# A fused attention and MLP kernel on one core gets a newly drawn order of work

## The chip, the cores and the metric

The kernel runs on one core of a Trainium2 chip. A core has five engines with instruction streams of their own: TensorE (PE, matrix products into the eight PSUM banks; its weight loads are shown as PEld), VectorE (DVE), ScalarE (ACT), GpSimd (POOL) and SyncE (SP). Each works through its stream in order and waits on semaphores where it needs another engine's result. The metric is device time in microseconds (us), lower is better. The median before is 210.59 us over three runs, from 210.03 to 211.24.

## The reference

Two stages follow each other. The first is a linear attention with decay: for each of 4 batches and 8 heads, 768 tokens of 64 elements are worked in blocks with a running state.

```python
intra = np.einsum('bhic,bhjc->bhij', qb, kb) * Dmask[None]
intra = np.einsum('bhij,bhjd->bhid', intra, vb)
inter = np.einsum('bhid,bhde->bhie', qb * lam_pow[None], kv_state)
out[:, :, sl] = intra + inter
kv_state = lam_block * kv_state + np.einsum('bhsd,bhse->bhde', kb * rev_pow, vb)
```

The second is an MLP on the 3072 tokens of 512 elements that come out, with 2048 hidden elements:

```python
h = x @ w_in
s = np.sin(alpha * h)
g = h + s * s / (alpha + 1e-09)
return (g @ w_out).astype(np.float32)
```

Inputs and output are float32 in memory; loads by POOL cast to bfloat16, and products accumulate in float32.

## The kernel before, in words

The tokens are cut into six tiles of 128 positions, each taken over all four batches: 512 rows to the MLP. A fixed opening (lines 148 to 454) loads tile 0 and works its attention. After it the whole program is a text of some 660 words, ORDER (line 16), which a loop (line 491) reads word by word; each word calls one step and so appends its instructions to the engines' streams. The order of the words is therefore the order on each engine; nothing reorders it later. A digit after a colon names the PSUM bank or banks that the step writes. The next user of a bank waits until its last reader is done.

The words, with t for a tile (g where the MLP uses it), f for a hidden block of 128 (0 to 15), m for a batch:

- Loads, issued by POOL: `I` (w_in, 512 of 2048 columns, two transfers, L141), `W` (w_out, a quarter, one transfer, L145), `r` and `R` (k and q of a tile in the layout that is to be turned, four transfers each, L124), `v` and `n` (v and k in natural layout, two transfers each, L131). r and R have a single buffer; the next load waits until the tile before is turned. w_in quarter 0 is loaded by the opening.
- POOL work: `d` (decay of k, L260), `z` (scaling of q, L264), `C` (cast of the first state).
- DVE work on the attention: `k`, `j` (turn k and q, L240), `m` (mask the scores, L255), `S` (new state, L283; tile 0's on ACT).
- PE work on the attention: `F` (scores, L249), `K` (state products, L274), `O` (outputs, L295 and L304).
- ACT work on it: `x` (copy of the outputs into the MLP's input, L314), `B` (cast of a state).
- The MLP: `h` (four matmuls for a hidden block, L325), `s` (sine on ACT, L330), `q` or `Q` or `P` (its square: on ACT, L336; on DVE as tensor_tensor, L338; on DVE as a three-operand operation, L340), `t` (DVE adds the scaled square to h from PSUM and writes g, which frees the bank, L345), `u` (four of the 16 matmuls of an output tile of 128 rows: `u0.1.2` is tile 0, batch 1, hidden blocks 8 to 11, L352), `o` (copy to SBUF on ACT, L358, and the store through SP, L360).

A tile's h need its four x; its u with part p need the t of blocks 4p to 4p+3 and w_out quarter p. The result blocks g of only two tiles exist at a time, so the first t of a tile waits for all u of the tile two before. After the last word, a call (line 494) makes the last output tile, tile 5 of batch 3, in two halves of 256 columns (L367), each copied (L371) and stored on its own.

Of the kernel before, what the change touches and what calls it, by code (L numbers as in the profile page):

```python
# [13 lines left out]


ORDER = """
I1 W0 d0.0 I2 h0.0:2 d0.1 h0.1:4 s0.0 h0.2:5 s0.1 Q0.0 I3 t0.0 K0:73 s0.2 Q0.1 h0.3:6 S0.0 r1 t0.1 q0.2 C0.0
h0.4:0 s0.3 t0.2 S0.1 h0.5:1 q0.3 h0.6:2 C0.1 s0.4 t0.3 s0.5 h0.7:7 R1 q0.4 u0.0.0:4 q0.5 t0.4 s0.6 u0.1.0:5
t0.5 s0.7 Q0.6 h0.8:3 t0.6 h0.9:6 Q0.7 s0.8 t0.7 h0.10:0 s0.9 Q0.8 t0.8 W1 h0.11:1 s0.10 Q0.9 W2 h0.12:2 t0.9
q0.10 s0.11 v1 t0.10 h0.13:7 s0.12 k1.0 h0.14:3 q0.11 q0.12 t0.11 h0.15:6 s0.13 W3 t0.12 s0.14 u0.2.0:0 k1.1  # L20
q0.13 z1.0 u0.3.0:1 q0.14 t0.13 s0.15 t0.14 q0.15 z1.1 j1.0 u0.0.1 t0.15 u0.1.1 j1.1 F1.0:2736 R2 u0.2.1 m1.0.0
m1.0.1 u0.0.2 m1.0.2 u0.1.2 m1.0.3 r2 F1.1:2736 u0.3.1 m1.1.0 m1.1.1 u0.2.2 m1.1.2 u0.3.2 m1.1.3 O1:2736 v2
u0.0.3 x1.0 x1.1 u0.1.3 x1.2 x1.3 u0.2.3 z2.0 o0.0 o0.1 h1.0:2 o0.2 h1.1:7 s1.0 z2.1 j2.0 h1.2:3 q1.0 k2.0 s1.1
h1.3:6 s1.2 n1 t1.0 h1.4:4 q1.1 k2.1 q1.2 u0.3.3 s1.3 t1.1 s1.4 h1.5:5 n2 t1.2 o0.3 h1.6:0 q1.4 P1.3 s1.5 t1.4
F2.0:2713 s1.6 t1.3 r3 h1.7:4 q1.5 m2.0.0 q1.6 h1.8:6 m2.0.1 s1.7 m2.0.2 u1.0.0:2 q1.7 m2.0.3 s1.8 d1.0 u1.1.0:7
t1.5 q1.8 h1.9:1 t1.6 t1.7 d1.1 h1.10:3 s1.9 t1.8 h1.11:5 q1.9 j2.1 s1.10 h1.12:0 d2.0 s1.11 t1.9 q1.10 K1:46
s1.12 t1.10 h1.13:1 d2.1 q1.12 S1.0 h1.14:3 s1.13 S1.1 B1.0 u1.0.1 t1.12 B1.1 R3 q1.13 Q1.11 K2:46 t1.11 s1.14
h1.15:0 t1.13 q1.14 u1.1.1 S2.0 s1.15 v3 u1.0.2 t1.14 q1.15 B2.0 S2.1 F2.1:5143 t1.15 B2.1 u1.1.2 m2.1.0 n3
u1.0.3 m2.1.1 m2.1.2 z3.0 u1.1.3 o1.0 m2.1.3 u1.2.0:6 o1.1 k3.0 O2:0514 z3.1 j3.0 k3.1 u1.3.0:2 x2.0 x2.1 j3.1
u1.2.1 x2.2 x2.3 F3.0:3705 h2.0:1 m3.0.0 m3.0.1 h2.1:4 s2.0 m3.0.2 h2.2:3 q2.0 m3.0.3 s2.1 t2.0 h2.3:7 s2.2 d3.0  # L30
u1.3.1 q2.1 q2.2 t2.1 h2.4:0 s2.3 t2.2 d3.1 h2.5:5 q2.3 s2.4 t2.3 h2.6:1 s2.5 r4 q2.4 K3:43 q2.5 t2.4 h2.7:7
s2.6 t2.5 h2.8:0 q2.6 S3.0 R4 s2.7 h2.9:5 t2.6 B3.0 s2.8 h2.10:4 Q2.7 t2.7 s2.9 h2.11:1 S3.1 q2.8 v4 q2.9 u1.2.2
t2.8 B3.1 t2.9 h2.12:7 s2.10 k4.0 s2.11 u1.3.2 n4 q2.10 k4.1 u1.2.3 q2.11 s2.12 u1.3.3 t2.10 o1.2 t2.11 q2.12
z4.0 F3.1:3054 o1.3 t2.12 u2.0.0:6 m3.1.0 h2.13:1 m3.1.1 z4.1 u2.0.1 m3.1.2 s2.13 m3.1.3 h2.14:2 j4.0 O3:7305
s2.14 Q2.13 q2.14 t2.13 t2.14 u2.0.2 x3.0 d4.0 j4.1 x3.1 h2.15:4 x3.2 x3.3 F4.0:1273 s2.15 d4.1 h3.0:0 m4.0.0
q2.15 m4.0.1 h3.1:5 s3.0 t2.15 h3.2:1 q3.0 m4.0.2 s3.1 t3.0 K4:24 s3.2 m4.0.3 u2.0.3 q3.1 S4.0 q3.2 h3.3:7 t3.1
o2.0 B4.0 u2.1.0:0 t3.2 r5 s3.3 S4.1 F4.1:3265 q3.3 u2.1.1 m4.1.0 B4.1 m4.1.1 h3.4:1 R5 m4.1.2 u2.1.2 m4.1.3
s3.4 t3.3 h3.5:4 q3.4 t3.4 v5 O4:3265 s3.5 k5.0 q3.5 u2.1.3 x4.0 t3.5 x4.1 k5.1 h3.6:7 x4.2 x4.3 h3.7:1 z5.0
o2.1 s3.6 u2.2.0:3 s3.7 h3.8:4 q3.6 z5.1 j5.0 q3.7 u2.2.1 s3.8 t3.6 F5.0:2650 q3.8 t3.7 u2.2.2 t3.8 h3.9:7
m5.0.0 m5.0.1 u2.2.3 s3.9 m5.0.2 h3.10:1 q3.9 m5.0.3 o2.2 u2.3.0:4 t3.9 s3.10 j5.1 h3.11:2 q3.10 t3.10 u2.3.1  # L40
s3.11 q3.11 F5.1:6503 u2.3.2 t3.11 m5.1.0 h3.12:7 m5.1.1 u2.3.3 m5.1.2 s3.12 m5.1.3 h3.13:1 q3.12 o2.3 t3.12
O5:2650 s3.13 q3.13 t3.13 u3.0.0:3 h3.14:4 u3.0.1 s3.14 h3.15:7 q3.14 t3.14 u3.0.2 x5.0 x5.1 h4.0:1 x5.2 x5.3
h4.1:4 s3.15 h4.2:2 s4.0 q3.15 h4.3:6 q4.0 t3.15 h4.4:5 s4.1 t4.0 s4.2 u3.0.3 q4.1 q4.2 h4.5:0 t4.1 o3.0 t4.2
u3.1.0:7 s4.3 s4.4 h4.6:1 q4.3 u3.1.1 q4.4 t4.3 s4.5 h4.7:4 t4.4 s4.6 u3.1.2 q4.5 q4.6 t4.5 h4.8:3 s4.7 t4.6
u3.1.3 q4.7 s4.8 t4.7 h4.9:2 o3.1 q4.8 u3.2.0:6 s4.9 t4.8 h4.10:5 q4.9 u3.2.1 t4.9 s4.10 u4.0.0:0 q4.10 t4.10
u3.2.2 h4.11:1 u3.2.3 s4.11 u4.0.1 q4.11 o3.2 t4.11 h4.12:4 u4.0.2 s4.12 h4.13:7 q4.12 t4.12 h4.14:3 s4.13
u4.1.0:2 q4.13 s4.14 t4.13 h4.15:5 q4.14 u4.1.1 t4.14 s4.15 h5.0:6 q4.15 t4.15 u4.1.2 s5.0 u4.0.3 q5.0 u4.1.3
o4.0 h5.1:1 o4.1 u3.3.0:4 s5.1 u4.2.0:7 q5.1 u3.3.1 h5.2:3 u3.3.2 s5.2 u4.2.1 q5.2 u3.3.3 h5.3:5 t5.0 o3.3
u4.2.2 t5.1 s5.3 t5.2 h5.4:0 q5.3 t5.3 u4.2.3 s5.4 h5.5:2 q5.4 o4.2 t5.4 u4.3.0:4 s5.5 h5.6:6 q5.5 t5.5 u4.3.1
s5.6 h5.7:1 q5.6 t5.6 u4.3.2 s5.7 h5.8:3 q5.7 t5.7 u4.3.3 s5.8 h5.9:5 q5.8 o4.3 t5.8 h5.10:7 s5.9 u5.0.0:0 q5.9  # L50
s5.10 t5.9 h5.11:2 q5.10 u5.0.1 t5.10 s5.11 h5.12:6 q5.11 t5.11 h5.13:1 s5.12 u5.0.2 q5.12 s5.13 t5.12 h5.14:4
q5.13 u5.1.0:3 t5.13 s5.14 h5.15:5 q5.14 t5.14 u5.1.1 s5.15 u5.2.0:7 q5.15 t5.15 u5.1.2 u5.0.3 u5.1.3 o5.0
u5.2.1 o5.1 u5.2.2 u5.2.3 o5.2
"""


# [1 line left out]
def kernel(  # L58
# [273 lines left out]
    def square(g, f, eng):  # L332
        s_sb = s_of.pop((g, f))
        s2_of[g, f] = mlps.tile([P, GRP], BF16, name="s2")
        if eng is A:
            A.activation(out=s2_of[g, f][:], in_=s_sb[:], func=ACTF.Square)  # L336
        elif eng is V:
            V.tensor_tensor(out=s2_of[g, f][:], in0=s_sb[:], in1=s_sb[:], op=ALU.mult)  # L338
# [9 lines left out]
    def project(g, m, part, n):  # L348
        if part == 0:
            ops[g, m] = bank("ops", n)  # L350
        for f in range(4 * part, 4 * part + 4):
            nc.tensor.matmul(out=ops[g, m][:], lhsT=gall[g][:, f, m * P:(m + 1) * P],  # L352
                             rhs=w_out_sb[part][:, f % 4, :],
                             start=(f == 0), stop=(f == NFC - 1))
# [170 lines left out]
```

## Time and profile before

| | us |
|---|---|
| median of three runs | 210.59 |
| the profiled execution, its own time | 212.47 |
| its span, first to last instruction | 210.8 |
| PE busy | 197.1 (94%) |
| DVE busy | 135.7 (64%) |
| ACT busy | 148.1 (70%) |
| POOL busy | 100.8 (48%) |
| last matmul ends | 207.57 |

The mean granted TensorE clock is 0.991 of full speed. POOL's own queue of loads moves 15.47 MB in 63184 packets; in the profile's 40 slices of 5.3 us the DMA engines are busy at nine tenths or more in twelve of the first thirteen. Busy time of PE is modelled for overlapping matmuls, so the waits and the order of time say more than the share. A row of a timeline gives start and length in us, engine, line, operation, tiles and a count; in brackets is the idle time ahead of it with what ended that.

### The profile page before, as it was taken

What the parts mean: (1) busy time and instruction counts of PE and PEld (TensorE: products, weight loads), DVE (VectorE), ACT (ScalarE), POOL (GpSimd) and SP (SyncE); (2) the same over time, 40 slices, a digit from 0 to 9 for tenths busy, and PEclk for the clock granted to TensorE, in tenths of its full rate; (3) what the DMA queues carried; (4) which work ended last, traced back from release to release, by engine and by line L of the source; (5) the groups of instructions that cost most, each with busy time, mean ns of one, the idle gap of its engine ahead of it and who ended that gap; (6) DMA issues with size and microseconds to landing.
All of it is one profiled execution on the core that took longest, in us unless ns stands there. A gap on an engine that the chain in (4) does not pass through costs nothing.

```text
span 210.8 us, 4860 instructions
## 1 busy us (share of the span) xinstructions
PE 197.1 (94%) x1992; PEld 97.7 (46%) x2021; DVE 135.7 (64%) x201; ACT 148.1 (70%) x258; POOL 100.8 (48%) x116
## 2 busy tenths in 40 slices
...
GB/s 124 156 151 182 205 193 162 165 197 166 229 165 166 77 145 183 48 142 157 157 75 166 116 53 50 51 2 0 53 50 50 0 100 35 70 16 33 0 105 98
DMA packets 68920, 22.61 MB, mean 107 GB/s; under 512 B 50834, under 2 KB 65954, under 8 KB 68898
## 3 DMA queue, kind: packets, MB, share of 16 engines
q0 software_dynamic: 63184, 15.47, 79.6%
...
q14 instruction: 6, 0.05, 0.1%
...
## 4 chain that ended last, share of the span: by engine, by line
PE 74%; DMA 11%; DVE 5%; POOL 4%; ACT 2%; issue 2%; DVEq 0%; ACTq 0%; POOLq 0%
PE ops L352 35%; PE hps L325 29%; DMA w_in<-in_moe_w_in_dram 4%; DMA w_out<-in_moe_w_out_dram 4%; DMA nat_k<-in_k_dram 3%; PE F_ps L249 3%; PE O_ps L304 2%; DVE gall L345 2%; POOL nat_k L260 2%; DVE STm L255 2%; PE hps L367 2%; PE O_ps L295 2%; POOL w_in L141 1%; DVE S L283 1%; PE T_ps L387 1%
## 5 line engine op out<-in xcount | busy, mean ns | idle before, releaser
L345 DVE SCALAR_TENSOR_TENSOR gall<-s,r_sb,hps 128x512 bf16<-128x512 bf16 x96 | 69.3, 742 | 46.9 <-ACT s L336 36.8
L325 PE MATMUL hps<-xt,w_in 128*128 128x512 bf16 x372 | 90.9, 379 | 2.0 <-issue 0.7
L352 PE MATMUL ops<-w_out,gall 128*128 128x512 bf16 x352 | 88.1, 382 | 4.0 <-DMA w_out<-in_moe_w_out_dram 2.4
L330 ACT ACTIVATE s_sb<-hps,alpha_sb 128x512 bf16<-128x512 f32 x96 | 64.2, 692 | 27.7 <-PE hps L325 27.5
L325 PEld LDWEIGHTS <-w_in 128*128 128x128 bf16 x384 | 36.7, 98 | 46.0 <-issue 2.2
L352 PEld LDWEIGHTS <-gall 128*128 128x128 bf16 x368 | 35.1, 98 | 44.8 <-issue 3.7
L336 ACT ACTIVATE s<-s_sb 128x512 bf16<-128x512 bf16 x86 | 52.9, 638 | 1.6
L255 DVE TENSOR_TENSOR STm<-F_ps,C 128x512 bf16<-128x512 f32 x40 | 25.0, 683 | 4.2 <-PE F_ps L249 4.1
L260 POOL TENSOR_TENSOR nat_k<-nat_k,R 128x1024 bf16<-128x1024 bf16 x10 | 19.1, 1933 | 4.5 <-DMA nat_k<-in_k_dram 4.4
L264 POOL TENSOR_TENSOR raw_q<-raw_q,Rraw 128x1024 bf16<-128x1024 bf16 x10 | 18.9, 1919 | 4.0 <-DMA raw_q<-in_q_dram 4.0
L314 ACT CAST xt<-O_ps 128x512 bf16<-128x512 f32 x20 | 10.3, 600 | 14.9 <-PE O_ps L304 14.5
L358 ACT COPY o_sb<-ops 128x512 f32<-128x512 f32 x23 | 13.5, 592 | 8.0 <-PE ops L352 6.2
L240 DVE STREAM_TRANSPOSE turned_q<-raw_q 128x512 f32<-128x512 f32 x10 | 11.1, 1114 | 5.6 <-POOL raw_q L264 5.6
L131 POOL DMA_DIRECT2D nat_v<-in_v_dram x12 | 14.0, 1170 | 0.2 <-issue 0.2
L124 POOL DMA_DIRECT2D raw_k<-in_k_dram x20 | 11.7, 598 | 3.9 <-DMA w_out<-in_moe_w_out_dram 2.9
L124 POOL DMA_DIRECT2D raw_q<-in_q_dram x20 | 11.6, 588 | 4.0 <-DMA w_in<-in_moe_w_in_dram 2.6
L131 POOL DMA_DIRECT2D nat_k<-in_k_dram x10 | 11.8, 1190 | 0.8 <-POOLq L509 0.8
L240 DVE STREAM_TRANSPOSE turned_k<-raw_k 128x512 f32<-128x512 f32 x10 | 11.0, 1117 | 0.1
L338 DVE TENSOR_TENSOR s<-s_sb 128x512 bf16<-128x512 bf16 x9 | 5.9, 657 | 2.4 <-ACT s_sb L330 2.4
L249 PEld LDWEIGHTS <-turned_k 32*128 32x128 bf16 x320 | 5.0, 96 | 4.6 <-issue 3.8
L249 PE MATMUL F_ps<-turned_q,turned_k 32*128 32x128 bf16 x320 | 6.8, 224 | 0.0
L192 PE MATMUL spare<-fill 128*128 128x512 bf16 x11 | 5.0, 607 | 1.5 <-DVE one L174 1.5
...
## 6 DMA issues: line engine op xcount, KB each, us to landing
...
```

Source lines behind the costliest of these rows:

```text
L124: (eng or G).dma_start(out=dst[quad[a], bs].rearrange("t b n r d -> t (b n) (r d)"), in_=src[t, a])
L131: G.dma_start(out=nat[nm, t][:, bs].rearrange("p b h e -> p (b h) e"), in_=SRC[nm][bs, :, t * T:(t + 1) * T, :].rearrange("b h p e -> p (b ...
L240: V.transpose(out=dst.rearrange("p (x t r) -> p x r t", r=R, t=32), in_=src.rearrange("p (x r d) -> p x r d", r=R, d=32))
L249: nc.tensor.matmul(out=F[a][:, u, n, :], lhsT=KQ["k", t][quad[a], 2 * pr + u, n, :, e], rhs=KQ["q", t][quad[a], 2 * pr + u, n, :, e], star ...
L255: V.tensor_tensor(out=st[t, pr][:, a], in0=att["F", pr][a], in1=C0[:, a].unsqueeze(1).broadcast_to([P, 2, NQ, T]), op=ALU.mult)
L260: G.tensor_tensor(out=kd, in0=kd, in1=R128[:].unsqueeze(1).unsqueeze(3).broadcast_to([P, 2, H, D]), op=ALU.mult)
L264: G.tensor_tensor(out=qs, in0=qs, in1=Rraw[:].rearrange("p n r -> p (n r)").unsqueeze(1).unsqueeze(3).broadcast_to([P, 2, NQ * R, D]), op= ...
L325: nc.tensor.matmul(out=hps[g, f][:], lhsT=w_in_sb[f // 4][:, c, (f % 4) * P:(f % 4 + 1) * P], rhs=xt[g][:, c, :], start=(c == 0), stop=(c ...
L330: A.activation(out=s_of[g, f][:], in_=hps[g, f][:], func=ACTF.Sin, scale=alpha_sb[:, f:f + 1])
L336: A.activation(out=s2_of[g, f][:], in_=s_sb[:], func=ACTF.Square)
L345: V.scalar_tensor_tensor(out=gall[g][:, f, :], in0=s2_of.pop((g, f))[:], scalar=r_sb[:, f:f + 1], in1=hps.pop((g, f))[:], op0=ALU.mult, op ...
L352: nc.tensor.matmul(out=ops[g, m][:], lhsT=gall[g][:, f, m * P:(m + 1) * P], rhs=w_out_sb[part][:, f % 4, :], start=(f == 0), stop=(f == NF ...
```

## The change

The table ORDER is another one, drawn by annealing over nine sets of disturbed durations. It has the same steps with the same numbers, so the same loads, matmuls, masks, sines, copies and stores, in other places and with other banks. The kinds of square differ: ACT had 86, DVE had 9 as tensor_tensor and 1 as three-operand operation; now ACT has 52, DVE 35 and 9. The output tile in halves becomes a word, `e5.3:14`, which gives its two banks; it still stands last. The fixed opening is untouched.

Of the diff, the start of both tables, the new part around tile 3's end, the new end, and the code:

```diff
 ORDER = """
-I1 W0 d0.0 I2 h0.0:2 d0.1 h0.1:4 s0.0 h0.2:5 s0.1 Q0.0 I3 t0.0 K0:73 s0.2 Q0.1 h0.3:6 S0.0 r1 t0.1 q0.2 C0.0
-h0.4:0 s0.3 t0.2 S0.1 h0.5:1 q0.3 h0.6:2 C0.1 s0.4 t0.3 s0.5 h0.7:7 R1 q0.4 u0.0.0:4 q0.5 t0.4 s0.6 u0.1.0:5
-t0.5 s0.7 Q0.6 h0.8:3 t0.6 h0.9:6 Q0.7 s0.8 t0.7 h0.10:0 s0.9 Q0.8 t0.8 W1 h0.11:1 s0.10 Q0.9 W2 h0.12:2 t0.9
-q0.10 s0.11 v1 t0.10 h0.13:7 s0.12 k1.0 h0.14:3 q0.11 q0.12 t0.11 h0.15:6 s0.13 W3 t0.12 s0.14 u0.2.0:0 k1.1
-q0.13 z1.0 u0.3.0:1 q0.14 t0.13 s0.15 t0.14 q0.15 z1.1 j1.0 u0.0.1 t0.15 u0.1.1 j1.1 F1.0:2736 R2 u0.2.1 m1.0.0
...
+h0.0:0 s0.0 I1 h0.1:2 s0.1 h0.2:6 s0.2 P0.0 q0.1 Q0.2 t0.0 t0.2 h0.3:7 s0.3 h0.4:4 q0.3 t0.3 t0.1 I2 h0.5:5
+h0.6:0 d0.1 h0.8:3 h0.7:2 s0.4 q0.4 t0.4 h0.10:4 s0.5 q0.5 d0.0 t0.5 s0.6 Q0.6 t0.6 s0.7 s0.8 P0.7 t0.7 Q0.8
+h0.9:5 s0.9 K0:70 Q0.9 t0.9 S0.0 I3 R1 W0 S0.1 s0.10 W1 t0.8 q0.10 t0.10 r1 W2 h0.11:1 s0.11 Q0.11 t0.11 h0.13:2
+W3 z1.0 h0.12:6 s0.12 s0.13 h0.14:5 q0.12 P0.13 z1.1 t0.12 h0.15:0 u0.1.0:7 s0.14 q0.14 u0.3.0:1 C0.1 u0.0.0:6
+u0.2.0:4 t0.13 j1.0 s0.15 q0.15 u0.3.1 t0.15 u0.0.1 j1.1 u0.2.1 k1.0 u0.1.1 t0.14 k1.1 F1.0:0532 u0.2.2 m1.0.2
+m1.0.0 v1 m1.0.1 m1.0.3 u0.1.2 u0.3.2 F1.1:0532 C0.0 m1.1.3 m1.1.1 u0.3.3 o0.3 u0.2.3 o0.2 m1.1.2 u0.0.2 m1.1.0
+O1:0345 x1.0 x1.1 u0.0.3 x1.3 x1.2 r2 k2.0 k2.1 u0.1.3 o0.1 R2 h1.0:5 s1.0 h1.1:1 h1.2:0 Q1.0 t1.0 o0.0 s1.1
+Q1.1 t1.1 s1.2 Q1.2 h1.3:4 t1.2 s1.3 q1.3 h1.4:6 h1.5:7 s1.4 s1.5 n1 t1.3 v2 h1.8:3 q1.4 q1.5 n2 z2.0 j2.0
...
+m3.0.2 m3.0.0 z3.1 u1.2.3 x2.3 h2.0:0 s2.0 m3.0.1 j3.1 Q2.0 t2.0 d3.0 h2.1:1 s2.1 q2.1 m3.0.3 h2.2:6 t2.1 h2.4:2
+h2.3:5 s2.2 s2.3 Q2.2 t2.2 s2.4 h2.5:4 o1.2 u1.3.0:1 Q2.3 h2.6:7 u1.3.1 Q2.4 t2.3 s2.5 d3.1 q2.5 v3 s2.6 q2.6
+t2.4 h2.7:3 F3.1:5026 s2.7 t2.5 q2.7 m3.1.1 h2.8:4 t2.6 u1.3.2 s2.8 q2.8 m3.1.3 h2.9:7 R4 s2.9 q2.9 u1.3.3
+m3.1.0 m3.1.2 K3:06 t2.7 S3.1 t2.9 o1.3 t2.8 B2.0 S3.0 r4 k4.0 h2.10:2 s2.10 z4.0 j4.0 h2.11:1 s2.11 O3:7356
+q2.10 q2.11 t2.10 t2.11 x3.0 x3.1 x3.2 u2.0.0:4 x3.3 h2.12:0 s2.12 Q2.12 t2.12 u2.0.1 F4.0:7652 m4.0.2 m4.0.3
...
+t5.14 u5.1.0:7 u5.2.2 u5.1.1 t5.15 u5.0.3 o5.0 u5.1.2 u4.0.0:0 u5.1.3 o5.1 u4.3.3 o4.3 u5.2.3 o5.2 u4.0.1 u4.0.2
+u4.0.3 o4.0 e5.3:14
 """
...
-    def project_halves(g, m):
+    def project_halves(g, m, *bks):
...
-            ps = bank("hps", n)
+            ps = bank("ops", bks[n])
...
+        "e": project_halves,
     }
     for word in ORDER.split():
         which, _, banks = word[1:].partition(":")
         STEP[word[0]](*map(int, which.split(".")), *map(int, banks))
-    project_halves(NT - 1, B - 1)
```

Of what the prediction names and the cut does not show: before, r4 stood ahead of R4 and v4, and v3 ahead of n3; the new order of loads from tile 3 on is R3 n3 z3 d3 v3 R4 r4 z4 n4 v4 d4 R5 r5 z5 v5.

More of the change, by code (lines that the diff above doesn't have):

```diff
@@ L22 @@
[L22 to L51, printed above, removed]
@@ L52 @@
-q5.13 u5.1.0:3 t5.13 s5.14 h5.15:5 q5.14 t5.14 u5.1.1 s5.15 u5.2.0:7 q5.15 t5.15 u5.1.2 u5.0.3 u5.1.3 o5.0
-u5.2.1 o5.1 u5.2.2 u5.2.3 o5.2
+h0.0:0 s0.0 I1 h0.1:2 s0.1 h0.2:6 s0.2 P0.0 q0.1 Q0.2 t0.0 t0.2 h0.3:7 s0.3 h0.4:4 q0.3 t0.3 t0.1 I2 h0.5:5
+h0.6:0 d0.1 h0.8:3 h0.7:2 s0.4 q0.4 t0.4 h0.10:4 s0.5 q0.5 d0.0 t0.5 s0.6 Q0.6 t0.6 s0.7 s0.8 P0.7 t0.7 Q0.8
+h0.9:5 s0.9 K0:70 Q0.9 t0.9 S0.0 I3 R1 W0 S0.1 s0.10 W1 t0.8 q0.10 t0.10 r1 W2 h0.11:1 s0.11 Q0.11 t0.11 h0.13:2
+W3 z1.0 h0.12:6 s0.12 s0.13 h0.14:5 q0.12 P0.13 z1.1 t0.12 h0.15:0 u0.1.0:7 s0.14 q0.14 u0.3.0:1 C0.1 u0.0.0:6
```

22 lines of the change are left out of this document (added).

## The prediction

> **What bounds the kernel now.** I read the busy shares first, then TensorE's groups, then TensorE in order of time, then clock and DMA by the microsecond, and last the single DMA issues.
>
> ```profile
> PE 197.1 (94%) x1992; PEld 97.7 (46%) x2021; DVE 135.7 (64%) x201; ACT 148.1 (70%) x258; POOL 100.8 (48%) x116
> ```
>
> TensorE (PE) is the only engine near its span. Its two large groups show what could still be won:
>
> ```profile
> L325 PE MATMUL hps<-xt,w_in 128*128 128x512 bf16 x372 | 90.9, 379 | 2.0 <-issue 0.7
> L352 PE MATMUL ops<-w_out,gall 128*128 128x512 bf16 x352 | 88.1, 382 | 4.0 <-DMA w_out<-in_moe_w_out_dram 2.4
> ```
>
> The last columns are idle time ahead of the group: little, and its largest piece is a wait for a w_out load. In order of time (start, length, matmuls):
>
> ```profile
> 34.21 1.89 PE L352 MATMUL ops<-w_out,gall 128*128 128x512 bf16 x8
> 38.49 2.37 PE L352 MATMUL ops<-w_out,gall 128*128 128x512 bf16 x8 [2.39 <-DMA w_out<-in_moe_w_out_dram]
> ...
> 42.16 3.04 PE L352 MATMUL ops<-w_out,gall 128*128 128x512 bf16 x11 [0.34 <-issue]
> ...
> 52.70 4.48 PE L325 MATMUL hps<-xt,w_in 128*128 128x512 bf16 x20
> ```
>
> Behind the wait the same matmuls are slower: eight took 2.37 us, against 1.73 in the chain. The rows by the microsecond say why (after the window: PE, PEld, DVE, ACT, POOL busy, then granted clock, DMA share, GB/s):
>
> ```profile
> 37.00:38.00 1.00, 0.00 (x0) 0.00 (x0) 0.51 (x1) 0.06 (x1) 1.00 (x2) 1.00 0.98 146
> ...
> 40.00:41.00 1.00, 1.00 (x14) 0.22 (x16) 0.44 (x1) 0.00 (x0) 0.27 (x1) 0.50 2.36 158
> 41.00:42.00 1.00, 0.82 (x32) 0.69 (x26) 0.15 (x1) 0.00 (x0) 1.00 (x3) 0.50 2.44 163
> 42.00:43.00 1.00, 0.84 (x2) 0.29 (x2) 1.00 (x2) 0.00 (x0) 1.00 (x2) 0.50 2.03 180
> ```
>
> The clock stood at half from about 39.2 to 43.1. Late in the run the chain is unbroken matmuls:
>
> ```profile
> 162.55 1.73 PE hps L325 x8
> 164.28 0.86 PE ops L352 x4
> ```
>
> So an h or u word of the table (four matmuls) costs 0.86 us of PE. By the chain an F is 0.57, an O 0.69 + 1.01 = 1.70, a K 0.62.
>
> **The ledger of before.** Words ahead of h1.0: 16 h, 15 u, K0, two F, O1, or 30.2 us. PE ran its first h at 16.79 and h1.0 at 52.70, 35.9 us; so 5.7 were lost: 2.39 for W1, some 1.7 at half clock (0.64 and 0.67 in the two rows above, 0.4 in the F between), the rest in short waits for w_in, K0 and banks. From h1.0 on there are 152.8 us of words and 154.87 us until 207.57, when PE ends: 2.1 lost, about 1.4 of it in gaps of 0.05 to 0.16 marked issue. The 3.2 us left are the last copy and store. The change removes no matmul, so it acts on 5.7 and 2.1 alone.
>
> **The change, part one: the opening.** The table moves W0 from between I1 and I2 to behind R1, and W1, W2 and W3 ahead of v1. POOL now issues I1, I2, d0.1, d0.0, I3, R1, W0, W1, r1, W2, W3, z1.0, z1.1, C0.1, v1, C0.0, r2. In PE's order every h0 and K0 now stands before the first u.
>
> Landing times come from the single DMA issues of before, in us: I1 21.3, W0 23.6, I2 27.3, I3 29.6, r1 32.2, R1 34.9, W1 38.5, W2 41.5, v1 45.0, W3 47.6. The transfers follow each other without a gap: a w_in pair costs 2.3 (27.3 to 29.6), four raw loads 2.6, a w_out 2.6 to 3.6 (I take 3.2), a nat pair 3.5. POOL's issues wait only for the load eight issues back (a raw_k issue at 23.8 went when W0 landed), which fits here. From I1 at 21.3 the new sequence gives I2 23.7, I3 26.1, R1 28.7, W0 32.0, W1 35.2, r1 37.8, W2 41.0, W3 43.8, v1 47.3.
>
> PE against that, each word 0.86: h0.0 at 16.79; h0.2 waits 0.2 for the second half of w_in (18.7); h0.4 waits 0.9 for I1; then 12 h and K0 (banks freed in time by rows of 0.70 per sine, 0.63 per square, 0.66 per finish) end at 32.3, when W0 is there. Eight u end at 39.4, behind W1. F1.0 waits 0.2 for DVE (z1.0 done 31.6, then j1.0, t0.15, j1.1, k1.0 after r1, t0.14); u0.2.2 waits 0.8 for W2; F1.1 waits 0.1 for masks. W3 and v1 are in time for u0.3.3 and O1. After O1 (48.5) four x copies (2.05 in before) hold h1.0's third matmul, 0.3. That is some 2.4 lost against 5.7: gain 3.3. No wait is above 0.9, so I take no clock drop. Bounds: with w_out at 3.6 each, and a square that meets z1.1 (below), 2.0; with 2.6 each, 4.2. I take 3.3, since 3.2 is the middle of the four w_out.
>
> The Trainium skill (TensorE: Matmul & The Clock Gate, Part 1) puts the drop after an idle window of about 3.4 us. This trace disagrees: 2.39 us sufficed. By that page the half clock would not belong to the W1 wait and the gain would be an estimated 1.6; I go by the row.
>
> **Part two: squares move from ACT to DVE.** Squares on ACT (q) fall from 86 to 52, on DVE as tensor_tensor (Q) they rise from 9 to 35, as the three-operand form (P) from 1 to 9. ACT sheds 34 x 0.615 = 21 us, DVE takes 26 x 0.42 + 8 x 0.68 = 16 us. After tile 3 both have room. Between h1.0 and h3.0 DVE's words sum to about 52 us beside 51 us of PE (before: 51 beside 53), so there the cover is gone. The price of a Q is not fixed:
>
> ```profile
> L338 DVE TENSOR_TENSOR s<-s_sb x9: 418/419/1824, 18.6 to 103.1; 128x512 bf16<-128x512 bf16 x9
> ```
>
> The 1.82 one began at 18.57, 0.4 after a POOL tensor_tensor (18.17 to 20.10), and ended as that one did; one at 103.06 took 1.16 beside another. Beside DMA issues it stays at 0.42. So a Q that meets a z or d loses up to 1.4. In the new order that can happen to Q0.11 (z1), Q1.2 (z2.0, about 55), Q2.0 (d3), Q3.7 (z5). Each delays DVE, and PE only where a bank is due: from 0 to 1.9 in all; I take 0.5. Denser bank reuse (h1.6 to u1.0.0 after 2.3 us of PE, where sine, square and finish need 0.69 + 0.63 + 0.75 + 0.2) adds 0 to 0.9; I take 0.3.
>
> **Part three: later loads.** r4 moves from ahead of R4 to behind v3 and R4, while k4.0 stands on DVE ahead of j4.0, t2.10 and t2.11, which F4.0 awaits. POOL after d3.1 (about 83.0) issues v3, R4, r4 until 90.0. From an empty queue n1 and n2 of before (54.7 to 59) took 5.5 us to the first landing, then 1.7 to 2.6 each, raw 0.65 to 1.0 each: r4 lands between 96.2 and 98.2. DVE is ready near 95.5 and PE wants F4.0 at 98.7; k4.0, j4.0 and t2.10 take 2.8, so F4.0 waits 0.3 to 2.3. I take 0.8, nearer the lower, which starts from an empty queue as here. K4 (d4.0 done 108 to 111, wanted 111.3) and F5.0 have little room: 0 to 1; I take 0.1.
>
> **Part four: the end.** project_halves becomes word e5.3 with banks 1 and 4 in place of 0 and 1; four u4.0 parts stand just ahead of it where u5.2 stood. Same matmuls, copies, stores: 0, bounds 0.3 either way.
>
> **Sum.** -3.3 + 0.5 + 0.3 + 0.8 + 0.1 = -1.6. The profiled execution took 212.47 (span 210.8 and 1.67 around it), so it would take 210.9; it lies 1.88 above the median of 210.59, so that I predict 209.0.
>
> **Rivals.**
> 1. All later terms hidden, since PE still has 152 us of words that banks may cover: 210.59 - 3.3 = 207.3. For it: DVE idles 4.7 us at 48 to 53 in before. Against: DVE was without a pause from 62 to 82.
> 2. DVE becomes the bound from tile 1 to 3: two or three squares meet POOL's operations at 1.4 each with nothing idle behind, 2.0 more than I took, and 210.9 or so. For it: 52 beside 51 us; against: 0.42 is what seven of nine took. The Trainium skill (SBUF — State Buffer, SBUF: two separate sides) extends the lock to any DVE operation with two SBUF inputs, so to P; no row here shows it for P.
> 3. Slower: r4 comes late. d3.0 waits for n3, v3 and R4 queue behind d3.1, r4 behind both, k4.0 blocks DVE, and PE stands at F4.0. Each us past 95.9 costs one. From a landing at 99.4 the kernel is over 0.5% slower; at 100 it takes 4.1 instead of 0.8 and gives 212.3. For it: R4 and r4 cost 4.0 and 3.1 us in before when the queue had run empty (issues at 88.7 and 86.35), against the 2.6 of the opening; against: the queue is empty when v3 goes.
>
> **How the numbers follow.** Within 0.5% means 209.5 to 211.6, about what a measurement can tell from no change. Forecast: 0.42 (its own range 207.9 to 210.2; 0.32 faster, 0.10 same). Rival 1: 0.22, faster. Rival 2: 0.16 (0.02 faster, 0.12 same, 0.02 slower). Rival 3: 0.20 (0.17 slower, 0.03 same). Sum: 0.56 faster, 0.25 same, 0.19 slower. The range runs from 206.8, half a us inside rival 1 with the opening's better bound (207.3 less part of the 0.9 between 3.3 and 4.2), to rival 3 at 212.3; it leaves out about 1 in 10 on either side.
>
> **What would show it.** Right: no wait of PE above 1 us for w_out, no clock row at 0.50 between 30 and 50, W0 landing near 32 and W3 near 44, h1.0 at about 50.5; r4 landing by 97 and F4.0 at about 99.5; about 165 us of large matmuls unchanged. Wrong: a new half-clock row, h1.0 after 52, DVE without a pause from 52 to 105 with several Q near 1.8, or F4.0 more than 2 us behind u2.0.1.

## The result, and the profile after

The changed kernel takes 222.75 us in the median of six runs (220.75 to 226.02), the kernel before beside it 210.57 (209.55 to 211.24). The ratio is 1.056, with a 95% interval of 1.050 to 1.061: 12 us slower, where the prediction said 209.0. Runs of one kernel scatter here, some by several per cent, so every ratio below compares undisturbed runs alone, and a median stands beside its range.

The profiled execution took 222.6 us with a span of 220.8, so it stands for the median. Its busy shares and its costliest groups:

```profile
PE 198.2 (90%) x1995; PEld 97.3 (44%) x2021; DVE 159.4 (72%) x235; ACT 130.4 (59%) x224; POOL 101.0 (46%) x116
L325 PE MATMUL hps<-xt,w_in 128*128 128x512 bf16 x372 | 91.5, 386 | 10.3 <-DVE gall L345 7.4
L352 PE MATMUL ops<-w_out,gall 128*128 128x512 bf16 x355 | 85.8, 380 | 3.9 <-DVE gall L345 2.6
L338 DVE TENSOR_TENSOR s<-s_sb 128x512 bf16<-128x512 bf16 x35 | 25.7, 736 | 13.1 <-ACT s_sb L330 12.9
```

Over the whole run TensorE's matmuls cost nearly what they did (386 and 380 ns in the mean against 379 and 382). New are 10.3 us of idle time ahead of the h group, most of it ended by DVE's finish (t, L345), and a square on DVE that takes 736 ns in the mean where 420 were reckoned. The answer for line 338 gives least, median and most in ns:

```profile
L338 DVE TENSOR_TENSOR s<-s_sb x35: 404/424/6152, 20.2 to 198.4; 128x512 bf16<-128x512 bf16 x35
```

So the usual square did cost 0.42, and one took 6.15. TensorE in order of time (in brackets the idle time ahead of a row and what ended it):

```profile
32.84 1.02 PE L352 MATMUL ops<-w_out,gall 128*128 128x512 bf16 x4
36.18 1.02 PE L352 MATMUL ops<-w_out,gall 128*128 128x512 bf16 x4 [2.32 <-DVE gall L345]
...
52.79 6.21 PE L325 MATMUL hps<-xt,w_in 128*128 128x512 bf16 x28
66.38 3.57 PE L325 MATMUL hps<-xt,w_in 128*128 128x512 bf16 x8 [7.39 <-DVE gall L345]
```

Eight matmuls of h took 3.57 us behind the long wait, against 1.73 in the unbroken chain. The windows show why (after the window: PE, PEld, DVE, ACT, POOL busy, then granted clock, DMA share, GB/s):

```profile
55.00:60.00 5.00, 4.00 (x19) 1.71 (x18) 5.00 (x1) 2.59 (x5) 5.00 (x3) 1.00 2.13 205
60.00:65.00 5.00, 0.00 (x0) 0.00 (x0) 4.89 (x6) 2.41 (x4) 4.60 (x6) 0.70 2.30 173
65.00:70.00 5.00, 3.62 (x16) 1.10 (x19) 3.85 (x6) 1.32 (x3) 3.19 (x2) 0.50 1.06 114
70.00:75.00 5.00, 4.78 (x47) 2.41 (x45) 3.61 (x6) 3.64 (x7) 0.61 (x1) 0.77 0.01 1
```

DVE is busy for the whole of 55 to 60 with one instruction, POOL with three. In order of time, the rows of DVE and POOL around both waits of TensorE (rows of other engines are left out):

```profile
31.28 3.77 POOL L264 TENSOR_TENSOR raw_q<-raw_q,Rraw 128x1024 bf16<-128x1024 bf16 x2
31.55 3.79 DVE L338 TENSOR_TENSOR s<-s_sb 128x512 bf16<-128x512 bf16 x1
...
54.58 6.15 DVE L338 TENSOR_TENSOR s<-s_sb 128x512 bf16<-128x512 bf16 x1 [2.18 <-ACT s_sb L330]
54.76 1.97 POOL L264 TENSOR_TENSOR raw_q<-raw_q,Rraw 128x1024 bf16<-128x1024 bf16 x1
56.63 1.96 POOL L260 TENSOR_TENSOR nat_k<-nat_k,R 128x1024 bf16<-128x1024 bf16 x1
58.49 1.95 POOL L264 TENSOR_TENSOR raw_q<-raw_q,Rraw 128x1024 bf16<-128x1024 bf16 x1
60.33 2.35 POOL L124 DMA_DIRECT2D raw_k<-in_k_dram  x4
61.43 1.34 DVE L338 TENSOR_TENSOR s<-s_sb 128x512 bf16<-128x512 bf16 x1
```

The square of 3.79 us is Q0.11. It lies beside z1.0 and z1.1, which follow each other without a pause, and ends 0.29 behind them. The one of 6.15 is Q1.0, beside z2.0, d1.0 and z2.1, and ends 0.29 behind the third, while POOL issues DMAs. Behind Q1.0 on DVE stand t1.0, Q1.1, t1.1, Q1.2, t1.2 and t1.3; the last frees bank 4 for h1.6.

How tight that is can be counted. TensorE has 28 matmuls (h1.0 to h1.5 and h1.8) before it needs bank 4, and stood still from 58.99. From Q1.0's start at 54.58 that is a cover of 4.4 us. At the usual prices DVE needs 3 x 0.42 + 4 x 0.75 = 4.3 us for these seven words. It took 11.8 (to 66.34), and 11.8 - 4.4 is the wait of 7.4. There was next to no slack (0.1), so nearly every microsecond on DVE was one on TensorE.

**The ledger.** After h1.0 the kernel has 151.9 us of words (0.86 less than before, since one more u now stands ahead of h1.0). It took from 52.79 to 217.53, so 12.8 were lost where the profiled execution of before lost 2.1: 7.4 in the wait, some 1.8 in the row of 65 to 70 (half of 3.62) and 1.1 in that of 70 to 75 (0.23 of 4.78) by the clock, the rest in short gaps. Ahead of h1.0 the same u shifts before's 52.70 to 53.56, so the opening won 0.8 of the 3.3 forecast. The sum, 10.7 - 0.8 = 9.9, is the difference of the spans (10.0).

### The profile page after: what moved, and what is told of

Read it like the earlier page. It is cut to its first block, busy times and chain, and to the rows that moved or that the text cites. A ratio compares the mean times of both kernels' runs of the same rounds, so it can differ in the third digit from the quotient of the medians.

```text
span 220.8 us, 4860 instructions
## 1 busy us (share of the span) xinstructions
PE 198.2 (90%) x1995; PEld 97.3 (44%) x2021; DVE 159.4 (72%) x235; ACT 130.4 (59%) x224; POOL 101.0 (46%) x116
## 4 chain that ended last, share of the span: by engine, by line
PE 67%; POOL 12%; DMA 12%; issue 3%; DVE 3%; ACT 0%; POOLq 0%; ACTq 0%; DVEq 0%
PE hps L325 30%; PE ops L352 30%; DMA nat_k<-in_k_dram 5%; DMA raw_k<-in_k_dram 4%; DMA w_in<-in_moe_w_in_dram 3%; POOL w_in L141 2%; PE F_ps L249 2%; POOL nat_v L131 2%; POOL nat_k L131 2%; PE O_ps L304 2%; PE ops L367 2%; POOL raw_k L124 2%; POOL nat_k L260 2%; PE O_ps L295 1%; PE KV_ps L274 1%
## 5 line engine op out<-in xcount | busy, mean ns | idle before, releaser
L325 PE MATMUL hps<-xt,w_in 128*128 128x512 bf16 x372 | 91.5, 386 | 10.3 <-DVE gall L345 7.4
L352 PE MATMUL ops<-w_out,gall 128*128 128x512 bf16 x355 | 85.8, 380 | 3.9 <-DVE gall L345 2.6
L345 DVE SCALAR_TENSOR_TENSOR gall<-s,r_sb,hps 128x512 bf16<-128x512 bf16 x96 | 68.7, 738 | 13.7 <-ACT s L336 12.6
L325 PEld LDWEIGHTS <-w_in 128*128 128x128 bf16 x384 | 37.2, 99 | 55.6 <-issue 13.3
L338 DVE TENSOR_TENSOR s<-s_sb 128x512 bf16<-128x512 bf16 x35 | 25.7, 736 | 13.1 <-ACT s_sb L330 12.9
L336 ACT ACTIVATE s<-s_sb 128x512 bf16<-128x512 bf16 x52 | 31.8, 628 | 1.0
L131 POOL DMA_DIRECT2D nat_k<-in_k_dram x10 | 11.8, 1186 | 1.5 <-POOLq L509 0.8
L340 DVE SCALAR_TENSOR_TENSOR s<-s_sb 128x512 bf16<-128x512 bf16 x9 | 7.0, 776 | 3.3 <-ACT s_sb L330 3.3
L283 DVE SCALAR_TENSOR_TENSOR S<-S,L,KV_ps 128x512 f32<-128x512 f32 x8 | 6.0, 745 | 3.3 <-PE KV_ps L274 3.3
(68 smaller groups left out, 101.4 us busy)
```

The costliest lines, as they stand in the source:

```text
L131: G.dma_start(out=nat[nm, t][:, bs].rearrange("p b h e -> p (b h) e"), in_=SRC[nm][bs, :, t * T:(t + 1) * T, :].rearrange("b h p e -> p (b ...
L325: nc.tensor.matmul(out=hps[g, f][:], lhsT=w_in_sb[f // 4][:, c, (f % 4) * P:(f % 4 + 1) * P], rhs=xt[g][:, c, :], start=(c == 0), stop=(c ...
L345: V.scalar_tensor_tensor(out=gall[g][:, f, :], in0=s2_of.pop((g, f))[:], scalar=r_sb[:, f:f + 1], in1=hps.pop((g, f))[:], op0=ALU.mult, op ...
```

## The experiments

The theories have letters in the expectations. **L**: a DVE square gets no turn while POOL's tensor_tensor operations follow each other without a pause (such a row is called a train below). Rivals are **W** (DVE simply has too much work), **D** (the later loads hold DVE and PE), **M** (only the two-operand form is held up) and, later, **O** (what the edited kernels still lack is lost in a stretch at half clock in the opening) and **S** against **T** (whether the wait for W1 is what put the profiled execution of before above the median, or is in every execution). The edits change only words of ORDER, so each kernel computes everything.

### Tile 1's three squares to ACT

```diff
-O1:0345 x1.0 x1.1 u0.0.3 x1.3 x1.2 r2 k2.0 k2.1 u0.1.3 o0.1 R2 h1.0:5 s1.0 h1.1:1 h1.2:0 Q1.0 t1.0 o0.0 s1.1
-Q1.1 t1.1 s1.2 Q1.2 h1.3:4 t1.2 s1.3 q1.3 h1.4:6 h1.5:7 s1.4 s1.5 n1 t1.3 v2 h1.8:3 q1.4 q1.5 n2 z2.0 j2.0
+O1:0345 x1.0 x1.1 u0.0.3 x1.3 x1.2 r2 k2.0 k2.1 u0.1.3 o0.1 R2 h1.0:5 s1.0 h1.1:1 h1.2:0 q1.0 t1.0 o0.0 s1.1
+q1.1 t1.1 s1.2 q1.2 h1.3:4 t1.2 s1.3 q1.3 h1.4:6 h1.5:7 s1.4 s1.5 n1 t1.3 v2 h1.8:3 q1.4 q1.5 n2 z2.0 j2.0
```

> The changed kernel with the squares Q1.0, Q1.1 and Q1.2 as q (on ACT), nothing else. Theory L (a DVE square with two SBUF inputs gets no turn while POOL's tensor_tensor operations follow each other without a pause): the 6.15 us square is gone, with it PE's wait of 7.39 us and the half clock behind it (about 3 us), so 211 to 214 us. Rival W (DVE simply has too much work in tiles 1 to 3, wherever POOL is): 1.3 us of DVE work are taken away, so 220 to 222 us. Rival D (the later loads hold DVE and PE): no change, 222 to 223 us.

Measured: 216.07 us (213.66 to 216.81), ratio 1.024 (1.016 to 1.031). The long wait shrank from 7.39 to 1.25, and the clock stayed at 1.00 from 60 to 70:

```profile
62.26 1.89 PE L325 MATMUL hps<-xt,w_in 128*128 128x512 bf16 x8 [1.25 <-DVE gall L345]
```

Three words of 660 give back 6.7 of the 12.2 us. L forecast 211 to 214, so it was 2 us too hopeful. Of this h1.6's wait accounts for 1.25: ACT now does three squares more among its sines, and each finish ahead of it waited for one of them. The opening was slower too: in this trace h1.0 starts only at 54.80, 2.0 later than in the changed kernel's, though no word ahead of it differs: Q0.11 took 3.40 us here too (TensorE waited 2.35), and the granted clock was 0.72 from 15 to 20 and 0.77 from 35 to 40, where the changed kernel's trace has 1.00. So one execution's opening can differ from another's by some 2 us, and a single trace prices it no better than that.

### Tile 0's one square to ACT

```diff
-h0.9:5 s0.9 K0:70 Q0.9 t0.9 S0.0 I3 R1 W0 S0.1 s0.10 W1 t0.8 q0.10 t0.10 r1 W2 h0.11:1 s0.11 Q0.11 t0.11 h0.13:2
+h0.9:5 s0.9 K0:70 Q0.9 t0.9 S0.0 I3 R1 W0 S0.1 s0.10 W1 t0.8 q0.10 t0.10 r1 W2 h0.11:1 s0.11 q0.11 t0.11 h0.13:2
```

> The changed kernel with the one square Q0.11 as q. L: the 3.79 us square beside z1.0 and z1.1 goes, PE's wait of 2.32 us ahead of u0.3.0 too: 220 us or less; since tile 1 then starts some 2 us earlier, its first squares may run ahead of z2.0, and then it can be down to 212. W: 0.4 us of DVE work less, 222 us. D: 222 to 223 us.

Measured: 221.12 us (218.84 to 226.88), ratio 1.042 (1.034 to 1.049). By the ratio (1.042 of 210.59 is 219.4) L's 220 or less is met. The profiled execution was the longest of the four (226.88), so its rows show what can happen and not what the median is made of. With Q0.11 gone, the next square on DVE, P0.13, ran into z1.1 and took 2.19 in place of 0.68. Q1.0 took 7.26:

```profile
53.34 7.26 DVE L338 TENSOR_TENSOR s<-s_sb 128x512 bf16<-128x512 bf16 x1 [1.76 <-ACT s_sb L330]
54.65 1.96 POOL L264 TENSOR_TENSOR raw_q<-raw_q,Rraw 128x1024 bf16<-128x1024 bf16 x1
```

Here Q1.2 met a second train as well, of three decays, and took 5.15; TensorE waited 12.22 us. One square less on DVE thus left others in POOL's operations: where a square meets one is a matter of a microsecond.

### All four to ACT

The two edits together.

> The changed kernel with Q0.11, Q1.0, Q1.1 and Q1.2 as q. L: both trains of POOL operations meet no square any more, 12 us come back: 209 to 211.5 us, no row of granted clock at 0.50 after the opening. W: 219 to 222 us. D: 221 to 223 us.

Measured: 213.75 us (211.64 to 215.47), ratio 1.011 (1.004 to 1.019). h1.0 starts at 51.17, and behind the wait for h1.6 TensorE has no idle time to speak of until the end:

```profile
58.63 1.89 PE L325 MATMUL hps<-xt,w_in 128*128 128x512 bf16 x8 [1.25 <-DVE gall L345]
```

Ahead of h1.0 one wait of 1.50 us is left, and it is P0.13 again (2.14 us beside z1.1). So four words carry 9 of the 12 us, though L's figure (209 to 211.5) is missed by about 2; the profiled execution took 211.64. All other moves of the table, tile 3's late loads (rival 3) and DVE's load between tile 1 and 3 (rival 2) among them, are left in this kernel and show no wait.

### The kernel before, with one square on DVE

The fault planted in the other order, at the word that stands ahead of POOL's three decays there:

```diff
-F2.0:2713 s1.6 t1.3 r3 h1.7:4 q1.5 m2.0.0 q1.6 h1.8:6 m2.0.1 s1.7 m2.0.2 u1.0.0:2 q1.7 m2.0.3 s1.8 d1.0 u1.1.0:7
+F2.0:2713 s1.6 t1.3 r3 h1.7:4 q1.5 m2.0.0 q1.6 h1.8:6 m2.0.1 s1.7 m2.0.2 u1.0.0:2 Q1.7 m2.0.3 s1.8 d1.0 u1.1.0:7
```

> The kernel before with one square, q1.7, as Q1.7 on DVE, where POOL runs four decays without a pause (61.6 to 69.1 us). L: the square starts near 63.5 and ends only at about 69.4, some 5.9 us; PE runs out of banks for 3 to 6 us and may lose up to 2 more at half clock: 214 to 219 us. W: 0.42 us of DVE work more, 210.5 to 211.5 us. D: no change.

Measured: 212.49 us in ten runs (210.46 to 221.5), ratio 1.003 (0.998 to 1.009). The mechanism is there in the profiled run, of 213.83 us; its price in the time can't be told from nothing, and L's figure is missed:

```profile
60.19 4.13 DVE L338 TENSOR_TENSOR s<-s_sb 128x512 bf16<-128x512 bf16 x1
60.22 5.86 POOL L260 TENSOR_TENSOR nat_k<-nat_k,R 128x1024 bf16<-128x1024 bf16 x3
```

The square ended 0.29 behind the second of three decays, and not behind the third. The profile shows no pause between them: the third starts at 63.95, as the second ends, and takes 2.12 in place of 1.9. So here the square got its turn inside a train, which L does not allow, and the decay seems to have waited instead. The trace of before has such a case as well: its square at 103.06 ended 0.29 behind the first of two decays (102.03 to 103.93), and the second, from 103.94, took 2.03. More of them stand under part two below. A mask and four finishes stood behind the square on DVE, and in this execution TensorE waited 2.63 us for the mask and 0.85 for a finish, waits that neither trace of the unedited kernel has.

### POOL's train split, squares left on DVE

Only POOL's words move: z2.0 ahead of the load n2, and the load r3 up to n2, so that z2.0 and the decays are parted by DMA issues. All squares stay as in the changed kernel.

```diff
-Q1.1 t1.1 s1.2 Q1.2 h1.3:4 t1.2 s1.3 q1.3 h1.4:6 h1.5:7 s1.4 s1.5 n1 t1.3 v2 h1.8:3 q1.4 q1.5 n2 z2.0 j2.0
+Q1.1 t1.1 s1.2 Q1.2 h1.3:4 t1.2 s1.3 q1.3 h1.4:6 h1.5:7 s1.4 s1.5 n1 t1.3 v2 h1.8:3 q1.4 q1.5 z2.0 n2 r3 j2.0
...
-t1.10 s1.13 z2.1 j2.1 t1.11 q1.12 t1.12 h1.14:1 u1.0.1 r3 q1.13 t1.13 d1.1 K1:62 d2.0 S1.0 s1.14 u1.1.1 q1.14
+t1.10 s1.13 z2.1 j2.1 t1.11 q1.12 t1.12 h1.14:1 u1.0.1 q1.13 t1.13 d1.1 K1:62 d2.0 S1.0 s1.14 u1.1.1 q1.14
```

> The changed kernel with two of POOL's words moved, n2 and r3 (load issues) now between z2.0 and d1.0, so that the train z2.0, d1.0, z2.1 is broken after its first operation; every word of DVE, ACT and PE stays. L (a square waits until POOL pauses between tensor_tensor operations): Q1.0 takes at most 2.3 us in place of 6.15, PE's wait of 7.39 shrinks to below 3 and the half clock goes: 213 to 217 us. Rival W (too much DVE work): the work is the same, 222 us. Rival D (what the loads do here): r3 earlier by one operation, 221 to 223 us.

Measured: 214.44 us (213.86 to 218.06), ratio 1.016 (1.009 to 1.022).

```profile
53.39 1.90 POOL L264 TENSOR_TENSOR raw_q<-raw_q,Rraw 128x1024 bf16<-128x1024 bf16 x1 [0.52 <-DMA raw_q<-in_q_dram]
55.24 2.37 POOL L131 DMA_DIRECT2D nat_k<-in_k_dram  x2
56.28 0.42 DVE L338 TENSOR_TENSOR s<-s_sb 128x512 bf16<-128x512 bf16 x1 [3.44 <-ACT s_sb L330]
57.41 0.42 DVE L338 TENSOR_TENSOR s<-s_sb 128x512 bf16<-128x512 bf16 x1
57.58 2.33 POOL L124 DMA_DIRECT2D raw_k<-in_k_dram  x4
58.52 0.42 DVE L338 TENSOR_TENSOR s<-s_sb 128x512 bf16<-128x512 bf16 x1
```

This tells L from W. DVE has the same 235 operations, but its three squares now lie beside DMA issues at 0.42 each, and TensorE's wait of 7.39 is gone altogether. In part that was luck: h1.0 started 1.7 us later here (54.50), so that Q1.0 came behind z2.0 and not beside it. Q0.11 was left as it was (2.01 us of wait). D falls too: n2 is issued later than in the changed kernel (55.24 against 52.47), and the wait is gone nevertheless.

### Tile 1's three squares in the other DVE form

```diff
-O1:0345 x1.0 x1.1 u0.0.3 x1.3 x1.2 r2 k2.0 k2.1 u0.1.3 o0.1 R2 h1.0:5 s1.0 h1.1:1 h1.2:0 Q1.0 t1.0 o0.0 s1.1
-Q1.1 t1.1 s1.2 Q1.2 h1.3:4 t1.2 s1.3 q1.3 h1.4:6 h1.5:7 s1.4 s1.5 n1 t1.3 v2 h1.8:3 q1.4 q1.5 n2 z2.0 j2.0
+O1:0345 x1.0 x1.1 u0.0.3 x1.3 x1.2 r2 k2.0 k2.1 u0.1.3 o0.1 R2 h1.0:5 s1.0 h1.1:1 h1.2:0 P1.0 t1.0 o0.0 s1.1
+P1.1 t1.1 s1.2 P1.2 h1.3:4 t1.2 s1.3 q1.3 h1.4:6 h1.5:7 s1.4 s1.5 n1 t1.3 v2 h1.8:3 q1.4 q1.5 n2 z2.0 j2.0
```

> The changed kernel with Q1.0, Q1.1 and Q1.2 as P, the three-operand form on DVE, 0.26 us dearer each. L: it also reads two SBUF inputs, so it starves in the same way, P1.0 takes 5 us or more and the kernel stays at 221 to 225 us. Rival M (only the form that runs at 0.42 us takes the port that POOL uses): every P stays near 0.7 us, 212 to 215 us.

Measured: 223.22 us (222.05 to 223.51), ratio 1.057 (1.051 to 1.063), a wait of TensorE of 6.80.

```profile
55.83 5.12 DVE L340 SCALAR_TENSOR_TENSOR s<-s_sb 128x512 bf16<-128x512 bf16 x1 [3.44 <-ACT s_sb L330]
```

The three-operand form (0.68 alone) is held until the train ends as well (it ends 0.57 behind the last operation), so M falls. The finish t, the same operation with one input from PSUM, took its usual 0.75 even beside z1.0 (at 31.82 in the kernel with all four on ACT). This is what the Trainium skill (SBUF — State Buffer, SBUF: two separate sides) says of operations with two SBUF inputs, and the prediction had no row for it; now there is one.

### All five meetings to ACT, and the split with tile 0's two on ACT

The first kernel has Q0.11, Q1.0, Q1.1, Q1.2 and P0.13 on ACT. The second has POOL's train split as above, with Q0.11 and P0.13 on ACT and tile 1's squares on DVE.

> The kernel of x3 with P0.13 also as q, which beside z1.1 still took 2.14 us there and held PE 1.5 us ahead of u0.0.0. L: that wait goes, 1.5 us less than x3: 210 to 212.5 us, and no square above 0.8 us before tile 2. W: no change against x3's 213.75 us.

> Both cures together: POOL's train split as in x5, and Q0.11 and P0.13 as q. Tile 1's three squares stay on DVE and relieve ACT, which in x3 held h1.6 by 1.25 us. L: the squares cost at most 2.3 us each and mostly 0.42: 209 to 212 us, level with the kernel of x7 or below. W: 219 us or more. D: 219 us or more.

Measured: the first 212.16 us in 13 runs (211.4 to 221.35), ratio 1.004 (1.000 to 1.008); the second 213.03 in 12 runs (211.39 to 225.07), ratio 1.009 (1.006 to 1.013). In the first, where L's figure is met, the wait on P0.13 is gone and h1.6 waits 0.50. The second misses L's (209 to 212) by about 1: there Q1.1 met z2.0, which had waited for its load:

```profile
53.80 1.90 POOL L264 TENSOR_TENSOR raw_q<-raw_q,Rraw 128x1024 bf16<-128x1024 bf16 x1 [1.12 <-DMA raw_q<-in_q_dram]
53.96 2.02 DVE L338 TENSOR_TENSOR s<-s_sb 128x512 bf16<-128x512 bf16 x1
```

Neither beats the kernel before.

### One DVE square left in tile 1

Q1.1 and Q1.2 go to ACT, Q1.0 stays.

```diff
-Q1.1 t1.1 s1.2 Q1.2 h1.3:4 t1.2 s1.3 q1.3 h1.4:6 h1.5:7 s1.4 s1.5 n1 t1.3 v2 h1.8:3 q1.4 q1.5 n2 z2.0 j2.0
+q1.1 t1.1 s1.2 q1.2 h1.3:4 t1.2 s1.3 q1.3 h1.4:6 h1.5:7 s1.4 s1.5 n1 t1.3 v2 h1.8:3 q1.4 q1.5 n2 z2.0 j2.0
```

> The changed kernel with Q1.1 and Q1.2 as q, so that in tile 1 a single square of 0.42 us stays on DVE, the one that met POOL's train. L: this one square alone still takes about 6 us, PE still waits 5 us or more for a bank and falls to half clock: 218 to 222 us. W (it is the amount of DVE work that counts): within 1 us of x1's 216.07 us.

Measured: 217.91 us (215.7 to 219.53), ratio 1.030 (1.023 to 1.036).

```profile
55.92 5.14 DVE L338 TENSOR_TENSOR s<-s_sb 128x512 bf16<-128x512 bf16 x1 [3.42 <-ACT s_sb L330]
...
63.87 3.31 PE L325 MATMUL hps<-xt,w_in 128*128 128x512 bf16 x8 [3.53 <-DVE gall L345]
```

The mechanism is there in the profiled execution (219.11 us): one square of 0.42 held for 5.14, and a wait of 3.53 where the kernel with none has 1.25. But L's figures (a wait of 5 us or more, 218 to 222 us) are missed, and the time does not settle it: the ratio of 1.030 lies within the interval of the kernel with none (1.024, from 1.016 to 1.031), and two of the four runs, 215.70 and 216.71, are what W forecast. What one held square costs in time thus stays open. It costs less than the three of the changed kernel (1.056); there Q1.1 and Q1.2 took 1.34 and 1.43 behind it, each ahead of a finish.

### The split, with Q1.1 on ACT and two banks exchanged

The split kernel of above, with Q1.1 on ACT as well and banks 4 and 5 exchanged in every word from h1.6 on.

> The kernel of x8 with two more edits: Q1.1, which there met z2.0 and took 2.02 us, as q; and banks 4 and 5 exchanged from h1.6 on, so that h1.6 takes the bank of h1.0 and not of h1.3. L: no square above 0.8 us before tile 2, PE's wait of 1.33 us ahead of h1.6 goes: 1 to 1.5 us less than x8, 210.5 to 212 us, level with the kernel before. Theory O (a half-clock stretch of the opening, 15 to 23 us, which x7 and x8 show and the profiled run of the kernel before does not, holds the rest): where a run has no such stretch, 209 us or less.

Measured: 213.01 us in 12 runs (210.3 to 226.02), ratio 1.008 (1.004 to 1.013). h1.6's wait of 1.33 became 0.33, but the time did not follow: the ratio stands beside the 1.009 of the second kernel above, where 1 to 1.5 us less was forecast. Q1.2 now met z2.0 and took 1.73, and F2.0, which had no wait in that kernel, waits 0.51. O's figure (209 or less without a half-clock stretch) is not tested, since the one trace has such a stretch (0.76 and 0.89 from 15 to 25). No version found here is faster than the kernel before.

### Two second traces: the kernel before, and all five on ACT

That kernels without any meeting still did not gain the opening's 3.3 us left a question: were they there to be won? The 3.3 had been read from an execution 1.9 us above the median.

> The kernel before, unedited, for a second trace of it. The prediction took its opening gain of 3.3 us from one execution of 212.47 us, 1.9 above the median. Theory S: these 1.9 us are the wait for W1 and the half clock behind it, so an execution near 210.6 shows a wait for W1 under 1 us, no stretch at half clock between 38 and 44, and h1.0 starting at about 51; then only some 1.4 of the 3.3 us were there to be won against the median. Theory T: the wait for W1 is in every execution (2 us or more, half clock behind it, h1.0 at 52.4 to 53), and the 1.9 us came from somewhere else.

> The changed kernel with Q0.11, P0.13, Q1.0, Q1.1 and Q1.2 on ACT once more, for a second trace of it. Its first trace (213.67 us) had 1.8 us lost at half clock between 15 and 25 and a gap of 1.1 us inside O3. Theory O: these are the 1.6 us by which it lies above the kernel before; an execution of about 212 shows one of them smaller or gone. Theory S (the kernel before is faster in the median than in its trace) needs no such difference: h1.0 starts at about 51 in both kernels, and the two are alike from there on within 1 us.

Measured: 210.73 us for the first, one run. TensorE in order of time, and a window of it:

```profile
37.71 1.89 PE L352 MATMUL ops<-w_out,gall 128*128 128x512 bf16 x8 [1.57 <-DMA w_out<-in_moe_w_out_dram]
...
50.56 2.75 PE L325 MATMUL hps<-xt,w_in 128*128 128x512 bf16 x12
```

```profile
40.00:45.00 5.00, 4.81 (x61) 2.25 (x52) 3.83 (x7) 0.00 (x0) 3.83 (x7) 1.00 1.80 185
```

The wait for W1 is 1.57 instead of 2.39, no half clock follows, and h1.0 starts 2.14 us sooner. (Against that, its windows show 0.66 between 15 and 20, which the first trace lacks.) From there on the two traces of before are alike within 0.4. The wait is between S's figure (under 1) and T's (over 2), but the clock and h1.0 are as S has them: by these two traces the 1.9 us by which the profiled execution stood above the median lay in the very stretch that the change mends.

The second took 211.09 us, in one run too:

```profile
50.07 6.21 PE L325 MATMUL hps<-xt,w_in 128*128 128x512 bf16 x28
57.52 1.89 PE L325 MATMUL hps<-xt,w_in 128*128 128x512 bf16 x8 [1.24 <-DVE gall L345]
```

With the one u more ahead of h1.0, before's 50.56 compares as 51.42: between these two traces the new opening is 1.35 faster. After h1.0 this kernel loses 4.1 us against 2.4 of before, 1.24 of it at h1.6. The balance, +0.35, is the difference of the two times (0.36). O falls as far as the clock goes: a window at 0.66 between 15 and 20 us is in both of these traces, so it does not part the two kernels. The gap of 1.1 us inside O3, which the first trace of all five on ACT had (213.67 us), is absent here.

The answer for line 338 of this kernel is the short form of the whole case:

```profile
L338 DVE TENSOR_TENSOR s<-s_sb x31: 416/420/426, 21.6 to 187.0; 128x512 bf16<-128x512 bf16 x31
```

With five words moved, the other 31 tensor_tensor squares that the table put on DVE cost 0.42 to 0.43 each.

## Why the prediction was wrong

**What bounds the kernel** was read rightly: TensorE's waits decide, and after 120 us the two traces show the same unbroken chain.

**Part one, the opening.** Most landings came as reckoned: I1 21.3, I2 23.9, I3 26.6, R1 29.6, W0 32.9, W1 35.9, r1 38.0, W2 40.5, W3 43.3 and v1 46.9, none more than 0.9 off. No u waited long for w_out. Still the gain was 0.8 in place of 3.3, since Q0.11 stood beside z1.0 and z1.1 for 3.79 us and t0.11 behind it was due: the wait of 2.32. With Q0.11 and P0.13 both on ACT h1.0 starts at 50.80, 51.05, 50.63 and 50.07 in four traces. That is 2.5 to 3.5 ahead of the profiled execution (53.56), as forecast, but only 0.4 to 1.35 ahead of before's second trace (51.42). That the half clock in before belonged to the wait of 2.39 fits its second trace (1.57, no half clock), but the changed kernel waited 2.32 in its opening at full clock, so it is not shown. Of the signs named for a wrong forecast two came true, h1.0 after 52 and a new row at 0.50 (65 to 70), and a third in part: DVE ran without a pause from 54.58 to 68.5, not to 105.

**Part two, the squares: here the prediction failed.** The step is "a Q that meets a z or d loses up to 1.4". It was read from two squares that got in when one operation of POOL ended, and it took this for the price of any meeting. (One of them met a single operation; the other met the first of two and got in between.) The runs show that a square can be held until the whole train ends: 3.4 us lost over two operations, 5.7 over three. The mechanism and the place were named (z1, and z2.0 "about 55"; it began at 54.76), but the square that stood there was Q1.0, not Q1.2; Q2.0 and Q3.7 took 0.42. The other half of the step, "PE only where a bank is due: from 0 to 1.9 in all; I take 0.5", measured 7.4 + 2.3 and, by the clock, some 2.9 more. I had not counted the cover behind h1.0: 4.4 us of matmuls for 4.3 of DVE. Rival 2 had the right kind of event but the same 1.4.

The figure of 1.4 is real all the same. In four traces (tile 1's three squares or tile 0's one on ACT, the split with all squares left on DVE, one square left in tile 1) Q3.4 met both z5 and lost 1.3 to 1.5. The first of them:

```profile
119.09 3.94 POOL L264 TENSOR_TENSOR raw_q<-raw_q,Rraw 128x1024 bf16<-128x1024 bf16 x2 [2.03 <-DMA raw_q<-in_q_dram]
...
119.44 1.83 DVE L338 TENSOR_TENSOR s<-s_sb 128x512 bf16<-128x512 bf16 x1
```

The square ended 0.28 behind z5.0; z5.1 had followed without a pause and took 2.08. What parts such a meeting from Q1.0's is not shown. The trains that held a square to the end (both z1 in five traces, tile 1's three in four, three decays in one) started right behind DMA issues; those of z5, and the two decays in before, started behind a wait for a load. But the square planted in before, and P1.2 in the kernel with the other form (1.60, then a decay of 2.34), got in though their trains had not waited.

**Bank reuse**, taken at 0.3: in kernels without a square held in tile 1 h1.6 waits 0.5 to 1.25 where tile 1's three squares are on ACT, and not at all in the split one with three squares at 0.42 on DVE.

**Part three, r4 and F4.0**, taken at 0.8, and rival 3: not seen. With all four or all five on ACT no idle time stands ahead of F4.0 (at 101.9 and 101.4). **K4, F5.0 and the end**: nothing, as said.

**The sum.** A second error is independent of the first. The gain of 3.3 was taken from the profiled execution, and the result was then lowered by 1.88 to the median. But by the second trace of before these 1.88 us lay in the same opening, so they were counted twice. With its own later terms (1.7) and the 0.4 to 1.35 that four traces show, the sum against the median would have been 210.9 to 211.9: within 0.7% of no change, and about what the kernel without its meetings gave (212.16 and, in one run, 211.09).

**What stays open.** By the ratios the edited kernels without long waits lie 0.4 to 1.1% above before. Their five traces show in which half: up to h1.0 they win 0.25 to 1.35 against before's second trace, and after it they lose 3.4 to 6.0 us where the two traces of before lose 2.1 and 2.4. Of the difference 0.3 to 1.3 is the wait for h1.6; the rest is short gaps that have not been followed up. In the traces of all five on ACT (the first one) and of the last split there is a gap of 1.1 us inside O3 that nothing in the profile explains.
